# One adaLN decode block: three weight and cache loads merged away, and the matmuls without a reader changed from bf16 to f32

## The chip, the cores and the metric

The kernel runs on one core of a Trainium2 chip. The metric is the device time of one execution in microseconds (us). Before the change it is 187.02 us, the median of three runs (186.99 to 187.12).

## The reference, cut to what matters

Two tokens (B = 2, one position each) of width D = 640 go through an adaLN-conditioned block: a modulation vector, an attention step over the last W = 1024 positions of a cache (32 heads of Dh = 192), and a gated MLP of width F = 1536.

```python
mod = (silu(c) @ w_mod).reshape(2, 6, 1, 640)      # sa, ca, ga, sb, cb, gb
h = layernorm(x) * (1 + ca) + sa
q = (h @ wq)                                       # 640 -> 32*192
scores = einsum('bhqd,bhkd->bhqk', q, k) * Dh ** -0.5
o = einsum('bhqk,bhkd->bhqd', softmax(scores), v)
x = x + ga * (o @ wo)                              # 32*192 -> 640
h = layernorm(x) * (1 + cb) + sb
out = x + gb * ((gelu(h @ w_gate) * (h @ w_up)) @ w_down)
```

All inputs are bf16. Nearly all bytes are read once: 25.2 MB of K and as much of V, 7.9 MB each of wq and wo, 4.9 MB of w_mod, and 5.9 MB of the three MLP matrices.

## The kernel before, in words

**How it is scheduled.** The program is written out as one list of operations per engine. `_Sched` records each operation with the buffers it reads and writes; when the lists are emitted, an operation waits for the counters of those that it depends on. Each engine works through its list strictly in order, so the order in which the code below calls `S.op` and `S.dma` is the order on each engine. All transfers are issued by SP (SyncE), on one hardware queue, also in order: a transfer whose buffer is not yet free holds up all transfers behind it.

**Buffers.** `ring` has four slots of one tile each (a tile is 64 positions x 192 for each of 128 partitions, 3 MB); `r1` is large enough for wq, and later holds two tiles (slots 4 and 5), and later wo. `items` lists the cache transfers as (kind, batch, first tile, number of tiles, slot, semaphore). `load_kv(n)` issues the items up to n at that place of SP's list.

**Scores** (lines 554 to 561). For each batch b, tile t and half hf, VectorE multiplies the half tile of K in place by the query (`d_mul`, L465), TensorE sums over the head dimension with twelve matmuls against an identity matrix (`p_reduce`, L476), and VectorE reduces the rest from PSUM (`d_rows`, L483). Between the halves TensorE has `filler()`: matmuls whose result nobody reads (L454). They write bank 4, which nobody needs at that time.

**Weighted values.** After the two softmaxes VectorE makes a masked copy of the weights for each tile (`d_mask`, L511), and TensorE multiplies it with the V tile (`p_pv`, L523, 32 matmuls). Batch 1's last two V tiles go into slots 2 and 3, which held batch 0's first two V tiles: each is issued when the matmuls of the tile that it replaces are done.

**Projection and MLP.** `normalize` (L536, L540), `p_sel` (L548) and three transposes (L597) bring the attention output into the form `oT`. wo arrives in pieces of `WO_SPLIT` row groups out of 48; after each piece come its matmuls (L628), 4 for each row group. Then the second layer norm: its statistics need one f32 matmul (L369), and it ends in a transpose to `hT` (L358). Then gate (L646), up (L646), and down (L669) in pieces of `WD_SPLIT`, and the output.

**Matmuls without a reader.** `warm(n, bk)` puts n matmuls on TensorE's list, in bf16, 128 x 128 weights (`ident_b`) against 384 columns (`qbc`). `WO_WARM`, `WU_WARM` and `WD_WARM` say how many follow each piece, and there are fixed calls around `p_sel`, before gate, and before up. In all there are 120 of them.

The order around the V tiles, the layer norm and the MLP, as TensorE's list has it: PV of batch 1's four tiles, `p_sel(0)`, warm, `p_sel(1)`, warm, wo pieces each with their warm matmuls, statistics matmul, warm, gate, warm, up, warm, down in three pieces with warm after the first.

Of the kernel before, what the change touches and what calls it, by code (L numbers as in the profile page):

```python
# [103 lines left out]
def bass_adaLN_cond__sliding_block_cached__geglu_ffn__decode_kernel(  # L104
# [17 lines left out]
    _, H, Sk, Dh = A_k_cache.shape  # L122
# [9 lines left out]
    DN = D // NJ  # L132
# [21 lines left out]
    NS = 4  # L154
    SL = J * Dh
    WQ_SPLIT = [5]
    assert sum(WQ_SPLIT) == KT
    WO_SPLIT = [16, 16, 12, 4]
    OT_SPLIT = [16, 16, 16]
    assert sum(WO_SPLIT) == NT and sum(OT_SPLIT) == NT  # L160
    WU_SPLIT = [5]
    assert sum(WU_SPLIT) == KT
    WD_SPLIT = [6, 4, 2]
    assert sum(WD_SPLIT) == FT
    ND = 4

    WO_WARM = [0, 8, 0, 9]
    WU_WARM = [5]
    WD_WARM = [5, 0, 0]

    es = ExitStack()
    with es:
        S = _Sched(nc, es)
# [21 lines left out]
        def tile_f(slot, n=1):  # L195
            if slot < NS:
                return ring_f[:, slot * SL:(slot + n) * SL]
            return r1[:, (slot - NS) * SL:(slot - NS + n) * SL]
# [11 lines left out]
        qbc = sb("qbc", [P, 2, Dh], BF16)  # L210
        ident_b = sb("ident_b", [P, P], BF16)
        ident_f = sb("ident_f", [P, P], F32)
# [15 lines left out]
        modC = sb("modC", [P, 6, DN], F32)  # L228
# [19 lines left out]
        ps = es.enter_context(nc.psum_tensor("ps", [P, 8, 512], F32))  # L248
# [4 lines left out]
        BK_W = 4  # L253
# [5 lines left out]
        def bank(k):  # L259
            return ("bank", k)  # L260
# [4 lines left out]
        sem_wq = [S.sem("d_wq%d" % i) for i in range(len(WQ_SPLIT))]  # L265
        sem_wo = [S.sem("d_wo%d" % i) for i in range(len(WO_SPLIT))]
        sem_wg = S.sem("d_wg")
        sem_wu = [S.sem("d_wu%d" % i) for i in range(len(WU_SPLIT))]
        sem_wd = [S.sem("d_wd%d" % i) for i in range(len(WD_SPLIT))]
        sem_ring = [S.sem("d_ring%d" % i) for i in range(4)]  # L270
        sem_out = S.sem("d_out")

        def k_dma(dst, src):
            return lambda e: e.dma_start(dst, src)  # L274
# [5 lines left out]
        def dram_rows(v):  # L280
# [9 lines left out]
             reads=[("S", 0, 0, 0), ("S", 0, 0, 1), ("S", 0, 1, 0), ("S", 0, 1, 1)], writes=["ident_f"], name="ident_f")  # L290
        S.op("pool", lambda e: e.tensor_copy(out=ident_b[:, :], in_=ident_f[:, :]),
             reads=["ident_f"], writes=["ident_b"], name="ident_b")
# [3 lines left out]
             reads=["ident_f"], writes=["G32"], name="G32")  # L296
        S.op("dve", lambda e: e.tensor_reduce(out=M32[:, :], in_=ident_f[:, :].rearrange("p (h t) -> p h t", t=QP), axis=AX.X, op=ALU.add),
             reads=["ident_f"], writes=["M32"], name="M32")
# [3 lines left out]
             reads=["G32"], writes=["Bsel"], name="Bsel")  # L302
# [3 lines left out]
             reads=["M32"], writes=["DS"], name="DS")  # L306


        for b in range(2):
            S.op("dve", (lambda b: lambda e: e.tensor_copy(  # L310
                out=SEL[:, b, :, BS * b:P:SQ], in_=G32[:, :].rearrange("p (j m) -> p m j", m=HM)))(b),
                reads=["G32"], writes=["SEL"], name="SEL%d" % b)
        for b in range(2):
            for m in range(HM):
# [3 lines left out]
                    reads=["ident_f"], writes=["Qsel"], name="Qsel%d%d" % (b, m))  # L318
# [4 lines left out]
        def ring_keys(slot):  # L323
            return [half_key(slot, 0), half_key(slot, 1)]
# [9 lines left out]


        items = [("k", 0, 0, 2, 0, 0), ("k", 0, 2, 2, 2, 1), ("k", 1, 0, 2, NS, 2), ("k", 1, 2, 2, 0, 0), ("v", 0, 0, 2, 2, 1),
                 ("v", 0, 2, 2, NS, 2), ("v", 1, 0, 2, 0, 0), ("v", 1, 2, 1, 2, 1), ("v", 1, 3, 1, 3, 3)]
        place = {(kind, b, t0 + i): slot + i for kind, b, t0, nt, slot, _ in items for i in range(nt)}
        assert NTL == 4 and len(place) == 4 * NTL

# [3 lines left out]
        def load_kv(upto, deps=()):  # L344
            while keep["kv"] < upto:
                kind, b, t0, nt, slot, sm = items[keep["kv"]]
                cache = A_v_cache if kind == "v" else A_k_cache
                S.dma("sp", k_dma(tile_f(slot, nt),
                                  cache[b, :, K0:Sk, :].rearrange("h (q r) d -> h q r d", q=QP)[:, :, J * t0:J * (t0 + nt), :].rearrange("h q r d -> h q (r d)")),
                      sem_ring[sm], writes=[k for i in range(nt) for k in ring_keys(slot + i)], deps=deps, name="ld_%s%d_%d" % (kind, b, t0))  # L350
                keep["kv"] += 1
# [98 lines left out]
        def warm(n, bk):  # L450
            def f(e):
                last = None
                for _ in range(n):
                    last = e.matmul(ps[:, bk, 0:2 * Dh], lhsT=ident_b[:, :], rhs=qbc[:, :, :].rearrange("p b d -> p (b d)"),  # L454
                                    start=True, stop=True)
                return last
            if n:
                S.op("pe", f, reads=["ident_b", "qbc"], writes=[bank(bk)], name="warm")

        def filler(n=1):  # L460
            warm(n * ND, BK_W)

        def d_mul(b, t, hf):
            ks = slot_of("k", b, t)
# [66 lines left out]
        def normalize(b):  # L531
            for g in range(NJ):
                rows = slice(SQ * g, SQ * (g + 1))
                cols = slice((g % 2) * Dh, (g % 2 + 1) * Dh)
                if g % 2 == 0:
                    S.op("act", (lambda rows, cols: lambda e: e.activation(out=On[rows, b, :], in_=ps[rows, BK_O, cols], func=ACTF.Identity,  # L536
                                                                           scale=rden[rows, b:b + 1]))(rows, cols),
                         reads=[bank(BK_O), ("rden", b)], writes=[("On", b, g)], name="On%d_%d" % (b, g))
                else:
                    S.op("dve", (lambda rows, cols: lambda e: e.tensor_scalar(out=On[rows, b, :], in0=ps[rows, BK_O, cols],  # L540
                                                                              scalar1=rden[rows, b:b + 1], scalar2=None, op0=ALU.mult))(rows, cols),
                         reads=[bank(BK_O), ("rden", b)], writes=[("On", b, g)], name="On%d_%d" % (b, g))

        def p_sel(b):
            def f(e):
                last = None
                for m in range(HM):
                    last = e.matmul(ps[:, BK_H + m // 2, (m % 2) * Dh:(m % 2 + 1) * Dh], lhsT=SEL[:, b, m, :], rhs=On[:, b, :],  # L548
                                    start=(b == 0 and m % 2 == 0), stop=(b == 1), skip_group_check=True)
                return last  # L550
            S.op("pe", f, reads=["SEL"] + [("On", b, g) for g in range(NJ)], writes=[bank(BK_H + c) for c in range(NQC)], name="sel%d" % b)


        def scores(b, ta, tb):
            for t in range(ta, tb):
                for hf in range(2):
                    d_mul(b, t, hf)
                    filler()
                    p_reduce(b, t, hf)
                    if (b, t, hf) != (0, 0, 0):  # L560
                        d_rows(*((b, t, 0) if hf else (b, t - 1, 1) if t else (b - 1, NTL - 1, 1)))

        def weighted(b, ta, tb):
            for t in range(ta, tb):
                d_mask(b, t)
                p_pv(b, t)
# [10 lines left out]
        softmax(0)  # L577
        softmax(1)
        weighted(0, 0, 2)
        load_kv(9)  # L580
        weighted(0, 2, 4)
        normalize(0)
        for t in range(NTL):
# [2 lines left out]
            if t == NTL - 1:  # L586
                p_sel(0)
        normalize(1)
        warm(3, 1)
        p_sel(1)  # L590
        warm(6, 1)
        assert keep["kv"] == len(items)
        for c in range(NQC):
            move(("act", "dve")[c % 2], oc[:, QC * c:QC * (c + 1)], ps[:, BK_H + c, 0:QC], [bank(BK_H + c)], [("oc", c)], "oc%d" % c)
# [1 line left out]
        for i, nt in enumerate(OT_SPLIT):  # L596
            S.op("dve", (lambda t0, nt: lambda e: e.transpose(oT[:, t0:t0 + nt, :], oc.rearrange("p (q k) -> p k q", k=NT)[:, t0:t0 + nt, :]))(t0, nt),  # L597
                 reads=[("oc", c) for c in range(NQC)], writes=[("oT", t) for t in range(t0, t0 + nt)], name="oT%d" % i)
            t0 += nt

        wo_src = A_wo.rearrange("(p t) n -> p t n", t=NT)
        wo_of = [(sum(WO_SPLIT[:i]), sum(WO_SPLIT[:i + 1])) for i in range(len(WO_SPLIT))]
        for i, (ta, tb) in enumerate(wo_of):
# [5 lines left out]
              writes=["wg"], deps=r3_dead, name="ld_wg")  # L609
# [13 lines left out]
        for i, (ta, tb) in enumerate(wo_of):  # L623
            def f(e, ta=ta, tb=tb):
# [6 lines left out]
            S.op("pe", f, reads=[("wo", i)] + [("oT", t) for t in range(ta, tb)], writes=[bank(BK_M)], name="wo%d" % i)  # L631
            warm(WO_WARM[i], 1)

        S.op("dve", lambda e: e.tensor_tensor(out=lnt[:, 0, :], in0=ps[:, BK_M, 0:DN], in1=modC[:, 2, :], op=ALU.mult),
             reads=[bank(BK_M), ("modC", 0)], writes=[("lnt", 0)], name="ga_attn")
        S.op("dve", lambda e: e.tensor_tensor(out=X2[:, 0, :], in0=lnt[:, 0, :], in1=X2[:, 0, :], op=ALU.add),
             reads=[("lnt", 0)], writes=[("X2", 0)], name="x1")
        layer_norm("ln2", 1, 3)
        warm(12, 1)

        def ffn_gu(bk, wv, key, name, ka, kb):
            def f(e):
# [6 lines left out]
            S.op("pe", f, reads=["hT", key], writes=[bank(bk)], name="ffn_" + name)  # L649

        ffn_gu(BK_G[0], wg_v, "wg", "wg", 0, KT)
        warm(8, 1)
        S.op("act", lambda e: e.activation(out=gl, in_=ps[:, BK_G[0], 0:FN], func=ACTF.Gelu_apprx_tanh),
             reads=[bank(BK_G[0])], writes=["gl"], name="gelu")
        k0 = 0
        for ci, nk in enumerate(WU_SPLIT):
            ffn_gu(BK_G[1], wu_v, ("wu", ci), "wu%d" % ci, k0, k0 + nk)
            k0 += nk
            warm(WU_WARM[ci], 1)
        S.op("dve", lambda e: e.tensor_tensor(out=aC[:, :], in0=ps[:, BK_G[1], 0:FN], in1=gl, op=ALU.mult),  # L660
             reads=[bank(BK_G[1]), "gl"], writes=["aC"], name="geglu")
        to_contraction(aT[:, :, :], aC[:, :], FT, ["aC"], ["aT"], "aT")
        f0 = 0
        for ci, nf in enumerate(WD_SPLIT):
            def f(e, f0=f0, nf=nf):
# [6 lines left out]
            S.op("pe", f, reads=["aT", ("wd", ci)], writes=[bank(BK_C)], name="down%d" % ci)  # L672
            warm(WD_WARM[ci], 1)
            f0 += nf

        S.op("dve", lambda e: e.tensor_tensor(out=lnt[:, 1, :], in0=ps[:, BK_C, 0:DN], in1=modC[:, 5, :], op=ALU.mult),
             reads=[bank(BK_C), ("modC", 1)], writes=[("lnt", 1)], name="gb_y")
        S.op("dve", lambda e: e.tensor_tensor(out=sc[:, :], in0=lnt[:, 1, :], in1=X2[:, 0, :], op=ALU.add),
             reads=[("lnt", 1), ("X2", 0)], writes=["sc"], name="outC")
# [36 lines left out]
```

## Time and profile before

| | before |
|---|---|
| time, median of three runs | 187.02 us |
| the profiled execution: its own time | 187.01 us |
| its span, first to last instruction | 185.7 us |
| granted TensorE clock, mean | 0.915 of full speed |
| DMA: bytes, mean rate | 77.02 MB, 415 GB/s |
| VectorE busy | 106.6 us (57%) |
| TensorE matmuls busy | 117.2 us (63%) |
| warm matmuls (L454) | 24.7 us, 120 of 339 ns each |
| ScalarE busy, GpSimd busy | 13.9 us, 4.9 us |

The profile is of one execution. The 1.31 us between its span and its time lie outside the instructions. A line such as "L454 PE MATMUL" names the line of the kernel, the engine and the operation. "PEld" is the load of the stationary operand, which runs beside matmuls. The record of a matmul includes its way through the array, so that one record of 339 ns does not mean that the next starts 339 ns later. The granted clock is full (1.0) or half (0.5) at each moment of this trace.

### The profile page before, as it was taken

How to read it: one execution, taken by the hardware profiler on the slowest of the kernel's cores; microseconds unless marked ns; L12 is line 12 of the kernel's file. 1: busy time of each engine (PE TensorE's matmuls, PEld its weight loads, DVE VectorE, ACT ScalarE, POOL GpSimd, SP SyncE). 2: the span in 40 equal slices, each digit the busy share in tenths (PEclk: the TensorE clock that was granted, in tenths of full speed). 3: DMA queues.
4: the chain of work that ended last, by engine and by line, in shares of the span. 5: the costliest groups of instructions: out<-in, count | busy, mean ns of one | idle time of the engine just before them, and what ended most of it. 6: DMA issues, size and time to landing. Idle time of an engine off the chain costs nothing.

```text
span 185.7 us, 2254 instructions
## 1 busy us (share of the span) xinstructions
PE 117.2 (63%) x1014; PEld 60.8 (33%) x1014; DVE 106.6 (57%) x114; ACT 13.9 (7%) x24; POOL 4.9 (3%) x12
## 2 busy tenths in 40 slices
PE   0004500871079899988999885349928977299844
PEld 0001200440024334433344342226614654265422
DVE  6801600020598999999999993294556714803331
ACT  2001400013000000000000000200010004100400
POOL 8200000000000000000000000000000000000000
PEclk9999999998559999999999999558996999859999
DMA  7999998898999989899999989899999999999991
GB/s 248 414 437 477 463 463 389 371 491 371 487 413 434 468 381 459 381 487 402 455 424 434 459 381 466 381 487 413 395 434 424 424 435 424 413 408 435 422 392 50
DMA packets 2925, 77.02 MB, mean 415 GB/s; under 512 B 356, under 2 KB 356, under 8 KB 868
## 3 DMA queue, kind: packets, MB, share of 16 engines
q1 hardware_dynamic: 2916, 76.88, 96.7%
q8 instruction: 8, 0.13, 0.3%
q14 instruction: 1, 0.01, 0.0%
HBM read 76.88 MB, written 0.00 MB: 414 GB/s over the span
## 4 chain that ended last, share of the span: by engine, by line
DMA 43%; DVE 36%; PE 16%; SPq 1%; ACT 1%; issue 1%; POOL 1%; DVEq 0%; POOLq 0%
DMA ring<-in_A_k_cache_dram 24%; DVE ring L465 19%; DMA ring<-in_B_w_down_dram 18%; PE ps L523 10%; DVE r L465 7%; DVE Sg L483 5%; PE ps L476 4%; DVE Em L511 2%; SPq L274 1%; ACT E_sb L502 1%; PE ps L504 1%; PE ps L498 1%; DVE On L540 0%; ACT On L536 0%; PE ps L491 0%
## 5 line engine op out<-in xcount | busy, mean ns | idle before, releaser
L465 DVE TENSOR_TENSOR ring<-ring,qbc 128x6144 bf16<-128x6144 bf16 x12 | 40.1, 3351 | 8.4 <-DMA ring<-in_A_k_cache_dram 8.4
L476 PE MATMUL ps<-ring,ident_b 128*128 128x512 bf16 x144 | 34.7, 393 | 13.0 <-DVE ring L465 13.0
L454 PE MATMUL ps<-qbc,ident_b 128*128 128x384 bf16 x120 | 24.7, 339 | 0.7 <-ACT qbc L432 0.7
L523 PE MATMUL ps<-ring,Em 128*64 128x384 bf16 x192 | 19.6, 371 | 7.8 <-DVE Em L511 6.6
L476 PEld LDWEIGHTS ps<-ring,ident_b 128*128 128x128 bf16 x144 | 13.6, 100 | 32.7 <-DVE ring L465 17.2
L511 DVE TENSOR_TENSOR Em<-E_sb,M32b 128x2048 bf16<-128x2048 bf16 x8 | 18.1, 2288 | 5.5 <-PE ps L523 5.5
L523 PEld LDWEIGHTS ps<-ring,Em 128*64 128x64 bf16 x192 | 12.4, 125 | 14.6 <-DVE Em L511 7.3
L454 PEld LDWEIGHTS ps<-qbc,ident_b 128*128 128x128 bf16 x120 | 11.6, 101 | 10.9 <-issue 2.8
L401 PE MATMUL ps<-ring,scT 128*32 128x480 bf16 x40 | 4.4, 601 | 16.0 <-DVE scT L358 16.0
L465 DVE TENSOR_TENSOR r<-r,qbc 128x6144 bf16<-128x6144 bf16 x4 | 13.4, 3352 | 0.0
L483 DVE TENSOR_REDUCE Sg<-ps 128x32 f32<-128x512 f32 x16 | 11.0, 687 | 3.4 <-PE ps L476 3.4
L424 PE MATMUL ps<-r,hT 128*32 128x384 bf16 x80 | 5.8, 475 | 10.7 <-DMA r<-in_A_wq_dram 10.7
L476 PE MATMUL ps<-r,ident_b 128*128 128x512 bf16 x48 | 11.1, 380 | 1.8 <-DVE r L465 1.8
L434 DVE CAST aux<-ps 128x384 bf16<-128x384 f32 x4 | 2.0, 553 | 16.6 <-PE ps L424 15.7
L628 PE MATMUL ps<-r,aux 128*32 128x160 bf16 x192 | 5.1, 271 | 4.4 <-DMA r<-in_A_wo_dram 2.6
L424 PEld LDWEIGHTS ps<-r,hT 128*32 128x32 bf16 x80 | 3.2, 135 | 13.8 <-issue 11.6
L476 PEld LDWEIGHTS ps<-r,ident_b 128*128 128x128 bf16 x48 | 4.4, 98 | 8.1 <-DVE r L465 3.4
L401 PEld LDWEIGHTS ps<-ring,scT 128*32 128x32 bf16 x40 | 1.2, 132 | 17.5 <-DVE scT L358 16.0
L540 DVE TENSOR_SCALAR On<-ps,rden 32x192 bf16<-32x192 f32 x4 | 1.7, 418 | 8.9 <-ACT On L536 8.9
L502 ACT ACTIVATE E_sb<-Sg,nb 128x256 bf16<-128x256 f32 x2 | 1.0, 507 | 75.6 <-DVE nb L501 75.6
L628 PEld LDWEIGHTS ps<-r,aux 128*32 128x32 bf16 x192 | 4.3, 114 | 5.8 <-DMA r<-in_A_wo_dram 3.6
L523 PE MATMUL ps<-r,Em 128*64 128x384 bf16 x64 | 5.4, 327 | 0.0
(73 smaller groups left out, 65.6 us busy)
## 6 DMA issues: line engine op xcount, KB each, us to landing
ring<-in_A_k_cache_dram SPq DMA_DIRECT2D x3, 6144.0 KB, 40.3
ring<-in_A_v_cache_dram SPq DMA_DIRECT2D x2, 6144.0 KB, 23.3
r<-in_A_wq_dram SPq DMA_DIRECT2D x1, 7680.0 KB, 30.7
r<-in_A_k_cache_dram SPq DMA_DIRECT2D x1, 6144.0 KB, 38.4
r<-in_A_v_cache_dram SPq DMA_DIRECT2D x1, 6144.0 KB, 23.3
ring<-in_A_v_cache_dram SPq DMA_DIRECT2D x2, 3072.0 KB, 17.6
r<-in_A_wo_dram SPq DMA_DIRECT2D x2, 2560.0 KB, 23.7
ring<-in_w_mod_dram SPq DMA_DIRECT2D x1, 4800.0 KB, 14.2
```

The lines of the kernel that those rows point to most:

```text
L274: return lambda e: e.dma_start(dst, src)
L401: last = e.matmul(ps[SQ * j:SQ * j + SQ, bk, 0:3 * DN].rearrange("p (i n) -> p i n", i=3), lhsT=scT[:, k, :], rhs=wm_v[:, k, 3 * part * D: ...
L424: last = e.matmul(ps[SQ * j:SQ * j + SQ, BK_H + c, 0:QC], lhsT=hT[:, k, :], rhs=wq_v[:, k, RN * j + QC * c:RN * j + QC * (c + 1)], start=( ...
L434: S.op("dve", lambda e: e.tensor_copy(out=dst, in_=src), reads=reads, writes=writes, name=name)
L454: last = e.matmul(ps[:, bk, 0:2 * Dh], lhsT=ident_b[:, :], rhs=qbc[:, :, :].rearrange("p b d -> p (b d)"), start=True, stop=True)
L465: S.op("dve", lambda e: e.tensor_tensor(out=tile_v(ks)[:, hf * JH:(hf + 1) * JH, :], in0=tile_v(ks)[:, hf * JH:(hf + 1) * JH, :], in1=qbc[ ...
L476: last = e.matmul(o_ap, lhsT=ident_b[:, :], rhs=tile_v(ks)[:, hf * JH:(hf + 1) * JH, ci * GC:(ci + 1) * GC], start=(ci == 0), stop=(ci == ...
L483: S.op("dve", lambda e: e.tensor_reduce(out=S_sb[:, b, a:a + JH], in_=ps[:, hf, 0:JH * GC].rearrange("p (j c) -> p j c", j=JH), axis=AX.X, ...
L502: S.op("act", lambda e: e.activation(out=E_sb[:, b, :], in_=S_sb[:, b, :], func=ACTF.Exp, scale=SCALE, bias=nb[:, 0:1], accum_out=esum[:, ...
L511: S.op("dve", lambda e: e.tensor_tensor(out=Em[:, t % 2, :, :], in0=E_sb[:, b, J * t:J * (t + 1)].unsqueeze(2).broadcast_to([P, J, H]), in ...
L523: last = e.matmul(ps[r:r + 2 * H, BK_O, 0:ON], lhsT=Em[:, t % 2, 2 * jp:2 * jp + 2, :].rearrange("p j c -> p (j c)"), rhs=tile_v(vs)[:, 2 ...
L628: last = e.matmul(ps[SQ * j:SQ * j + SQ, BK_M, 0:DN], lhsT=oT[:, t, :], rhs=wo_v[:, t, DN * j:DN * j + DN], start=(t == 0), stop=(t == NT ...
```

## The change

It does three things.

1. Batch 1's last two V tiles come in one transfer of 6 MB into slots 2 and 3 in place of two of 3 MB. It is issued when both tiles that it replaces are done, and both of its tiles wait for all of it.
2. wo comes in two pieces, of 32 and 16 row groups, in place of four of 16, 16, 12 and 4.
3. A matmul without a reader is now f32: 128 x 128 weights (`ident_f`) against 480 columns of `modC`. Four of the bf16 matmuls give way to one of these, with rounding: after the wo pieces 0, 8, 0, 9 become 2, 2; after up 5 becomes 1, after the first piece of down 5 becomes 1; the fixed calls go from 3, 6, 12 and 8 to 1, 1, 3 and 2; each of the 16 fillers between scores goes from four to one. In all 120 become 29.

```diff
-    WO_SPLIT = [16, 16, 12, 4]
+    WO_SPLIT = [32, 16]
...
-    ND = 4
-
-    WO_WARM = [0, 8, 0, 9]
-    WU_WARM = [5]
-    WD_WARM = [5, 0, 0]
+
+    WO_WARM = [2, 2]
+    WU_WARM = [1]
+    WD_WARM = [1, 0, 0]
...
-        sem_ring = [S.sem("d_ring%d" % i) for i in range(4)]
+        sem_ring = [S.sem("d_ring%d" % i) for i in range(3)]
...
-                 ("v", 0, 2, 2, NS, 2), ("v", 1, 0, 2, 0, 0), ("v", 1, 2, 1, 2, 1), ("v", 1, 3, 1, 3, 3)]
+                 ("v", 0, 2, 2, NS, 2), ("v", 1, 0, 2, 0, 0), ("v", 1, 2, 2, 2, 1)]
...
-                    last = e.matmul(ps[:, bk, 0:2 * Dh], lhsT=ident_b[:, :], rhs=qbc[:, :, :].rearrange("p b d -> p (b d)"),
+                    last = e.matmul(ps[:, bk, 0:3 * DN], lhsT=ident_f[:, :], rhs=modC[:, 0:3, :].rearrange("p i n -> p (i n)"),
...
-                S.op("pe", f, reads=["ident_b", "qbc"], writes=[bank(bk)], name="warm")
+                S.op("pe", f, reads=["ident_f", ("modC", 0)], writes=[bank(bk)], name="warm")
 
         def filler(n=1):
-            warm(n * ND, BK_W)
+            warm(n, BK_W)
...
-        load_kv(9)
+        load_kv(8)
...
-        warm(3, 1)
+        warm(1, 1)
         p_sel(1)
-        warm(6, 1)
+        warm(1, 1)
...
-        warm(12, 1)
+        warm(3, 1)
...
-        warm(8, 1)
+        warm(2, 1)
```

## The prediction

> **What bounds the kernel now.** I read the page first: which resource has no holes, and what the chain that ended last is made of. Columns of the slices: tenths of busy time in 40 slices; of the queue: packets, MB, share of 16 engines.
>
> ```profile
> DMA  7999998898999989899999989899999999999991
> q1 hardware_dynamic: 2916, 76.88, 96.7%
> DMA ring<-in_A_k_cache_dram 24%; DVE ring L465 19%; DMA ring<-in_B_w_down_dram 18%; PE ps L523 10%; DVE r L465 7%; DVE Sg L483 5%; PE ps L476 4%; DVE Em L511 2%; SPq L274 1%; ACT E_sb L502 1%; PE ps L504 1%; PE ps L498 1%; DVE On L540 0%; ACT On L536 0%; PE ps L491 0%
> ```
>
> The transfer engines are busy from the second slice to the last but one, and no compute engine is. The chain names VectorE and TensorE in the middle, but they only decide when SP may issue; it ends in a 33.92 us wait for the last piece of w_down. The second view is the chain in order of time, its end:
>
> ```profile
> 148.89 33.92 DMA ring<-in_B_w_down_dram
> 182.81 0.04 issue
> 182.85 0.35 PE ps L669 x8
> ```
>
> So the last byte lands at 182.81, and 2.9 us of the span follow. A change pays if the stream of transfers ends earlier, and costs if compute is not ready for its last piece. The third view is the timeline of the tail (start, us, engine line; in brackets the idle time before and who ended it):
>
> ```profile
> 150.84 2.79 PE L523 MATMUL ps<-ring,Em 128*64 128x384 bf16 x32 [1.14 <-DMA ring<-in_A_v_cache_dram]
> ...
> 162.78 2.33 PE L628 MATMUL ps<-r,aux 128*32 128x160 bf16 x64 [2.41 <-DMA r<-in_A_wo_dram]
> ...
> 169.00 0.46 PE L628 MATMUL ps<-r,aux 128*32 128x160 bf16 x16 [0.21 <-DMA r<-in_A_wo_dram]
> ...
> 171.37 2.11 PE L454 MATMUL ps<-qbc,ident_b 128*128 128x384 bf16 x12
> ...
> 174.09 1.00 PE L646 MATMUL ps<-ring,hT 128*32 128x384 bf16 x20 [0.61 <-DVE hT L358]
> 175.02 1.47 PE L454 MATMUL ps<-qbc,ident_b 128*128 128x384 bf16 x8
> ...
> 178.18 1.00 PE L646 MATMUL ps<-ring,hT 128*32 128x384 bf16 x20 [1.69 <-DMA ring<-in_B_w_up_dram]
> ```
>
> Every stage of the tail waits for a transfer; the tightest slack is the 1.69 us before up. The clock by stages (us; PE and PEld busy; clock in the column after POOL):
>
> ```profile
> 147.40:150.85 3.45, 2.31 (x32) 1.40 (x27) 2.06 (x1) 0.00 (x0) 0.00 (x0) 1.00 1.01 425
> 157.70:161.10 3.40, 1.29 (x64) 1.12 (x64) 3.40 (x3) 0.83 (x1) 0.00 (x0) 0.99 0.98 417
> 161.10:164.50 3.40, 1.72 (x55) 1.72 (x59) 0.51 (x1) 0.00 (x0) 0.00 (x0) 0.50 0.99 413
> ```
>
> 2.31 us of work in 3.45 kept the full clock; 1.29 in 3.40 was followed by half clock.
>
> **Three transfers fewer.** The trace's records of single packets (median duration) price them. Of a transfer's 128 packets an engine carries 8, then a semaphore packet of 9 ns. A V packet of 24,576 bytes takes 0.9155 us, one of 49,152 takes 1.816: the merge saves 8 x (2 x 0.9155 - 1.816) + 0.009 = 0.129 us. wo's 15,360 and 5,120 bytes take 0.577 and 0.198, 20,480 takes 0.766: 8 x 0.009 + 0.009 = 0.081. The 40,960-byte packet is not in the trace; between 38,400 bytes (1.420) and 49,152 it is 1.514: 8 x (2 x 0.766 - 1.514) + 0.009 = 0.153. Sum 0.36 us of each engine, and since the queue has no holes all of it moves the last landing. Bounds: 0.22 if the new packet size saves only its semaphore, 0.5 if an unseen few ns lie between packets.
>
> SP issues the merged V after batch 0's second tile, at about 130.6, where the first of the pair went out one tile (2.6 us) earlier. The transfer ahead, issued at 113.52, lands 23.3 us later (the page's median), at about 136.8, so the queue does not run dry: 5 us or more of cover. Behind it on SP stand the wo transfers, which are issued at 135.84 in any case.
>
> **Both V tiles wait for 150.8.** The third PV tile ran from about 147.1 beside the last landing; now it starts at 150.8 with the fourth. One tile is 2.4 us at full clock, 4.5 at half (the tile at 139.99, after 4.18 us of idling). TensorE now idles from 147.1 to 150.8, 3.7 us, so the first 3.4 us may run at half clock: PV ends at 155.9 to 157.3 instead of 153.6. Behind it TensorE's list holds `p_sel`, warm and wo. oT began 3.9 us after PV; two transposes (1.42 each) are needed for the first 32 groups: ready at 162.6 to 164.0. That wo piece lands where the second did, 162.7. So the merge is hidden, or costs 1.3 here.
>
> **wo in two pieces.** First piece: 128 matmuls at half clock (64 in 2.01) 4.0 us, to 166.6 to 168.0; two f32 matmuls to 168.2 to 169.7. The second lands at 168.95 - 0.36 = 168.6, and now has 64 matmuls (1.12 at full clock, 0.17 to the end of the last) where 16 were left: done at 170.0 to 171.0, against 169.46. This is 0.5 to 1.5 late into the layer norm, which nothing but the slack before up covers.
>
> **f32 matmuls.** The trace has none with many columns except the transposes of L491 (128 columns): 270 ns at full clock, 372 at half. The 102 ns between are twice what 128 bf16 columns would differ by (0.42 ns a column, from twelve 512-column matmuls in 2.60 us, against 0.83): two column times each. An f32 matmul that is no transpose is two records (L369: x4 for two calls). So 2 x 2 x 480 x 0.42 = 0.81 us, against 0.65 for four bf16. Below: 0.40, if a record streams at bf16's rate; above: 1.1, if its two weight loads (0.30 us the pair at 171.13) are not hidden, as bf16's are. I take 0.81, as L491 is the nearest row. Between scores a half has 2.60 of reduction in a VectorE period of 3.87, so 1.27 us are free: hidden at any of these prices.
>
> In the tail, on the path: the statistics come 1.62 after wo's end, 171.6 to 172.6; two f32 (1.6) fit. hT 2.9 later, at 174.6 to 175.5; three f32 (2.4) fit. Gate 0.93, two f32 1.6: up can start at 177.1 to 178.1. It lands at 178.15 - 0.36 = 177.8. From up's start to the last piece of down are 2.6 (geglu, transpose), 0.53, one f32 0.8, 0.35: 4.3, and that piece lands at 182.45: up may start as late as 178.15 at no cost. It fits with nothing to spare at the late end. **The sum:** the profiled execution has 187.01; minus 0.36 is 186.65, and the median 187.02 gives 186.66.
>
> **Rivals.**
> 1. *The f32 matmul takes 1.1 us (slower).* Decisive above about 0.9. From 164.0: wo to 168.0, two f32 170.2, wo's second 171.4, two f32 173.6 (statistics wait for them), 173.9, three f32 177.2 (past hT), gate 178.1, two f32 180.3, up 181.2, f32 182.3, aT at 182.9, down 0.53, f32 1.1, last 24 matmuls 0.5: 185.0 against 183.05 before. Some 1.9 us: 188.9. For it: f32 weight loads take 0.15 each at full clock, bf16's 0.08. Against: loads run ahead of the matmul before.
> 2. *The f32 matmuls hold the clock less (slower).* Then the tail runs at half clock from 164: f32 1.6 us each, wo's second piece 2.2, gate and up 1.8. The same sum ends near 193.5, 10 us late: 197; with the clock lost for one or two stretches of 3.4 us, 188 to 192. Against: between scores 2.6 of 3.87 us remain bf16, 67%, the share that held at 147.40. For it: from 174.70 to 178.15 the warm matmuls are most of the work. The Trainium skill (TensorE: Matmul & The Clock Gate, on the clock gate) has half clock after an idle window of some 3.4 us. The trace is stricter, since 1.29 busy of 3.40 was already too little; the late ends of the sum have the merged V tiles at half clock for that.
> 3. *Part of the slack is overrun.* At f32 0.9 or half clock at one more place, up starts 0.3 to 0.7 past 178.15: 186.8 to 187.3.
> 4. *Each transfer has a cost of its own on the path.* The Trainium skill (DMA: Bandwidth & Descriptors, on the anatomy of one DMA) gives about 2 us fixed per DMA on GpSimd's path, which for three would be an estimate of 6 us, 181 in all; the trace does not bear it out. As a mechanism here: gaps between transfers. The five from 169.00 to 182.81 carry 5.9 MB, 427 GB/s, so no such gap is seen. If there were 0.2 us at each, the time would be 186.66 - 0.6 = 186.1.
>
> **How the numbers follow.** 0.2% is 0.37 us, about what a measurement of this kernel can tell from no change. The forecast case (0.52) ends at 186.65 give or take 0.1, on that very bound: half faster, half the same. Rival 1 has 0.28, rival 2 0.08, rival 3 0.08 (same), rival 4 0.02, a score stage at half clock 0.02 (twelve matmuls 5.1 and f32 1.6 make 6.7 a half, 16 x 2.8 = 45 us on VectorE's chain, some 35 past the queue's backlog). Faster 0.27 + 0.02 = 0.29, same 0.25 + 0.08 = 0.33, slower 0.38. The likeliest case's own range is 186.5 to 186.8; the range to 188.9 takes in rivals 1 and 3 and leaves out some 0.13.
>
> **What would show it.** Right: the last w_down piece landing 0.3 to 0.4 earlier with 2916 - 3 x 144 = 2484 packets on q1; L454 records (58) starting 0.4 us apart in the tail; PV's last 64 in one run from 150.7; up still released by its transfer. Wrong: up or down released by TensorE's own list (L454 before them), a clock of 0.50 after 168, or a hole in the DMA row near 135.

## The result, and the profile after

The changed kernel takes 187.59 us, the median of 14 runs, from 187.25 to 189.39. The kernel before takes 187.14 beside it (186.88 to 187.26). It is slower by 0.45 us at the median, and far less even than before. The ratio of the means is 1.0040, with a 95% interval of 1.0026 to 1.0054. Such ratios, here and below, are of means, which a few long executions move more than a median, and they leave out executions over 1.5% above the fastest of their kernel. The profiled execution has 187.55, a span of 186.3, 0.6 more than before.

The page of the changed kernel, the lines that answer to those shown of before:

```profile
DMA  7999998899998989999898989989899999999980
q1 hardware_dynamic: 2484, 76.88, 96.3%
DMA ring<-in_A_k_cache_dram 25%; DVE ring L464 19%; DMA ring<-in_A_v_cache_dram 11%; PE ps L522 8%; DVE r L464 7%; DVE Sg L482 5%; PE ps L475 4%; PE ps L453 3%; PE ps L627 3%; DVE aux L596 2%; DVE Em L510 1%; PE ps L645 1%; ACT E_sb L501 1%; PE ps L503 1%; PE ps L668 1%
```

The packets went as counted (2484), but w_down, 18% of the chain before, is gone from it. In its place stand V (11%), the f32 matmuls (L453, 3%) and wo's (L627, 3%). The lines are one lower than before, since a line was removed. The chain in order of time, its end:

```profile
164.63 4.00 PE ps L627 x125
168.62 1.81 PE ps L453 x4
170.43 1.22 PE ps L627 x64
171.65 1.81 PE ps L453 x4
173.46 0.26 PE ps L368 x2
...
176.28 1.00 PE ps L645 x20
177.28 1.81 PE ps L453 x4
179.09 0.95 PE ps L645 x20
...
182.23 1.00 PE ps L453 x2
183.23 0.56 PE ps L668 x24
```

No transfer is left in this end: TensorE goes from piece to piece, and four groups of f32 matmuls (L453) stand among them. The timeline of TensorE where that run begins, the row of two tiles at full clock in the kernel before, and the line of the f32 matmuls of the changed kernel (min/median/max ns):

```profile
150.77 7.07 PE L522 MATMUL ps<-ring,Em 128*64 128x384 bf16 x64 [3.58 <-DMA ring<-in_A_v_cache_dram]
```

```profile
130.41 5.39 PE L523 MATMUL ps<-r,Em 128*64 128x384 bf16 x64
```

```profile
L453 PE MATMUL ps<-modC,ident_f x58: 566/566/670, 41.7 to 182.7; 128*128 128x480 f32 x58
```

The last two PV tiles start together after 3.58 us of idling and take 7.07 us, where two tiles took 5.39 in the kernel before, at a granted clock of 1.00. The last landing of w_down, at 183.13 by the trace, is 0.3 later than before, not 0.36 earlier, and yet TensorE is not waiting for it: its f32 matmuls end at 183.23. Had TensorE been ready, the last eight matmuls (0.35) would have ended at 183.5, where they ended at 183.20 before; they ended at 183.79. So of the 0.6 that the span grew, 0.3 is there by the stream alone, and the chain on TensorE, which sets the end, adds the rest.

### The profile page after: what moved, and what is told of

Read it like the earlier page. It is cut to its first block, busy times and chain, and to the rows that moved or that the text cites. A ratio compares the mean times of both kernels' runs of the same rounds, so it can differ in the third digit from the quotient of the medians.

```text
span 186.3 us, 2125 instructions
## 1 busy us (share of the span) xinstructions
PE 121.5 (65%) x952; PEld 61.9 (33%) x952; DVE 106.6 (57%) x114; ACT 13.9 (7%) x24; POOL 4.9 (3%) x12
## 3 DMA queue, kind: packets, MB, share of 16 engines
q1 hardware_dynamic: 2484, 76.88, 96.3%
## 4 chain that ended last, share of the span: by engine, by line
DVE 39%; DMA 35%; PE 21%; ACT 1%; issue 1%; POOL 1%; SPq 0%; DVEq 0%; POOLq 0%
DMA ring<-in_A_k_cache_dram 25%; DVE ring L464 19%; DMA ring<-in_A_v_cache_dram 11%; PE ps L522 8%; DVE r L464 7%; DVE Sg L482 5%; PE ps L475 4%; PE ps L453 3%; PE ps L627 3%; DVE aux L596 2%; DVE Em L510 1%; PE ps L645 1%; ACT E_sb L501 1%; PE ps L503 1%; PE ps L668 1%
## 5 line engine op out<-in xcount | busy, mean ns | idle before, releaser
L453 PE MATMUL ps<-modC,ident_f 128*128 128x480 f32 x58 | 28.0, 578 | 0.0
L522 PE MATMUL ps<-ring,Em 128*64 128x384 bf16 x192 | 21.2, 393 | 10.2 <-DVE Em L510 6.6
L522 PEld LDWEIGHTS ps<-ring,Em 128*64 128x64 bf16 x192 | 14.0, 132 | 17.1 <-DVE Em L510 7.1
L453 PEld LDWEIGHTS ps<-modC,ident_f 128*128 128x128 f32 x58 | 10.3, 190 | 5.3 <-issue 2.8
L627 PE MATMUL ps<-r,aux 128*32 128x160 bf16 x192 | 5.3, 289 | 3.3 <-DVE aux L596 3.3
L627 PEld LDWEIGHTS ps<-r,aux 128*32 128x32 bf16 x192 | 4.9, 124 | 4.7 <-issue 4.7
```

What stands on the lines that cost most here:

```text
L453: last = e.matmul(ps[:, bk, 0:3 * DN], lhsT=ident_f[:, :], rhs=modC[:, 0:3, :].rearrange("p i n -> p (i n)"), start=True, stop=True)
L522: last = e.matmul(ps[r:r + 2 * H, BK_O, 0:ON], lhsT=Em[:, t % 2, 2 * jp:2 * jp + 2, :].rearrange("p j c -> p (j c)"), rhs=tile_v(vs)[:, 2 ...
L627: last = e.matmul(ps[SQ * j:SQ * j + SQ, BK_M, 0:DN], lhsT=oT[:, t, :], rhs=wo_v[:, t, DN * j:DN * j + DN], start=(t == 0), stop=(t == NT ...
```

## The experiments

Each time stands beside runs of the kernel before on the same chip, whose medians were 187.00 to 187.08.

**The three edits apart.**

V's last two tiles in two transfers again, the rest as changed:

```diff
-                 ("v", 0, 2, 2, NS, 2), ("v", 1, 0, 2, 0, 0), ("v", 1, 2, 2, 2, 1)]
+                 ("v", 0, 2, 2, NS, 2), ("v", 1, 0, 2, 0, 0), ("v", 1, 2, 1, 2, 1), ("v", 1, 3, 1, 3, 3)]
```

> The changed kernel with V's last two tiles in two transfers again. Theory (the merged V sends both tiles to 150.8, TensorE idles into half clock, and from there an unbroken chain of TensorE and VectorE work sets the end): the chain is 4 us shorter, up waits for its transfer again, and the two wo transfers saved are left: 186.9, that is 0.2 below the kernel before (187.14). Rival (the f32 matmuls or the wo split cost the time by themselves): it stays at 187.4 to 187.6.

Measured 186.88 (186.77 to 187.16), ratio 0.9993 [0.9984, 1.0002]. Neither the f32 matmuls nor the wo split cost any time without the merged V. But the mechanism was not quite the expected one: in its profile up landed at 178.10 and started at 178.31, behind TensorE's own list, and only the last eight matmuls waited for their transfer again (182.76). The slack behind up took the 0.2.

bf16 matmuls in the changed kernel (8 and 9 behind wo's pieces, 3, 6, 12, 8, 5, 5 elsewhere):

```diff
-                    last = e.matmul(ps[:, bk, 0:3 * DN], lhsT=ident_f[:, :], rhs=modC[:, 0:3, :].rearrange("p i n -> p (i n)"),
+                    last = e.matmul(ps[:, bk, 0:2 * Dh], lhsT=ident_b[:, :], rhs=qbc[:, :, :].rearrange("p b d -> p (b d)"),
```

> The changed kernel with four bf16 matmuls of 384 columns for each f32 one. Theory: the chain from 150.8 remains, but it has four stations where two f32 take 1.81 against 1.3 of eight bf16, about 1.2 us less before up; up would be ready at 177.9, before its transfer (178.5): 186.8 to 187.1. Rival (the merged V alone is too late for any fillers): 187.4 or more.

Measured 187.78 (186.82 to 189.23), ratio 1.0050 [1.0025, 1.0075]. The theory fell here: without the f32 matmuls the median is no lower, and in the profiled execution (188.74) the chain ends in w_down, landing at 184.62. The stream itself was late, by 1.8 us. Three of the twelve executions (186.82, 187.12, 187.13) do lie below the lowest of the changed kernel (187.25), so bf16 may help where the stream is in time; this run does not show it.

V merged alone (point 1 of the change and nothing else), in the kernel before:

> The kernel before with only V's last two tiles merged. Theory: PV ends at 157.8, wo's end is 0.7 late, and the slack before up (1.7 us) takes it: 187.0, 0.1 below the kernel before, with more spread. Rival (the merge alone costs it): 187.4 or more.

Measured 187.80 (186.78 to 189.90), ratio 1.0036 [1.0013, 1.0059]. The rival holds: the merge alone costs this much, and it makes executions differ by 3 us.

wo in two pieces alone:

```diff
-    WO_SPLIT = [16, 16, 12, 4]
+    WO_SPLIT = [32, 16]
...
-    WO_WARM = [0, 8, 0, 9]
+    WO_WARM = [8, 9]
```

> The kernel before with only wo in 32 and 16 (eight and nine bf16 matmuls behind the pieces). Theory: the last piece has 64 matmuls behind it in place of 16, 0.85 us, taken by the slack before up; the stream ends 0.23 earlier by the packet prices: 186.9. Rival A (64 matmuls behind the last piece show): 187.4 or more. Rival B (the last landing is set by the slowest of 16 engines and does not move by what is saved on the mean engine): 187.1.

Measured 186.87 (186.71 to 187.04), ratio 0.9990 [0.9981, 0.9998]: 0.13 less than the runs beside it, between the theory (0.23 less) and its rival B (nothing).

The f32 matmuls alone (point 3):

> The kernel before with only the f32 matmuls (wo in four pieces with 0, 2, 0, 2 behind them). Theory: 0.9 us each against 0.65, hidden between scores and in the slack of the tail: within 0.1 of the kernel before. Rival (the f32 matmuls cost the time by themselves): 187.4 or more.

Measured 186.89 (186.76 to 187.09), ratio 0.9994 [0.9985, 1.0002]. They have no cost of their own.

**What a transfer costs.** wo in 24 transfers:

```diff
-    WO_SPLIT = [16, 16, 12, 4]
+    WO_SPLIT = [2] * 24
...
-    WO_WARM = [0, 8, 0, 9]
+    WO_WARM = [0] * 15 + [8] + [0] * 7 + [9]
```

> The kernel before with wo in 24 transfers of two row groups. It measures the price of a transfer: by the packet prices wo takes 24 x (8 x 0.102 + 0.009) = 19.8 us of each engine in place of 18.5, and the end comes 1.3 us later: 188.4. Rival (a transfer has no price on the path): 187.1. Rival (each costs far more, 0.5 us or so): 197.

Measured 188.47 (188.26 to 188.54), ratio 1.0078 [1.0065, 1.0091]: 1.4 us for 20 transfers more, where the packet records say 1.3.

**TensorE's part.** Four f32 matmuls where TensorE waits for the merged V:

```diff
                 p_pv(1, t)
+            if t == 1:
+                warm(4, 1)
```

> The changed kernel with four f32 matmuls more, behind the second PV tile of batch 1, where TensorE waits 3.6 us for the merged V. Theory: the last two PV tiles run at full clock and end at about 155.7 in place of 157.8, wo's first piece starts on its transfer, and the chain is off the path: 186.9 to 187.1. Rival (half clock there is not what makes the chain late): 187.4 or more.

Measured 187.21 (186.83 to 189.26), ratio 1.0031 [1.0007, 1.0055]. In the profiled execution (187.01) the two tiles took 5.39 and up waited for its transfer again, as the theory has it. But the median is 0.1 above what it gave, and the spread did not go.

No matmuls behind the wo pieces (`WO_WARM = [0, 0]`):

> The changed kernel without the f32 matmuls behind the two wo pieces (two and two left out; nobody reads them). Theory: they stand in the chain, 1.8 us behind the first piece and 0.2 in front of the statistics, so up is ready 1.8 or more earlier and waits for its transfer: 186.9 to 187.1. Rival (they keep the clock): wo's second piece and what follows run at half clock, 187.6 to 189.

Measured 188.27 (186.82 to 190.65), ratio 1.0047 [1.0022, 1.0072]. A miss, and mixed with the lateness below. The profile shows the rival's mechanism: a granted clock of 0.64 from 172 to 176, where the changed kernel has 1.00. So the two pairs left out here hold the clock; in the changed kernel the same pairs stand in the chain.

**The late stream.** The packets of the merged V showed what the theory lacked. In the kernel before, the 16 transfer engines finish the V transfer ahead one by one, from 133.6 to 135.4; the next one was issued at 128.0. With V merged it is issued at 130.8 to 132.0, and in the profiled executions of five kernels with it 3 to 21 packets from 133 to 139 took 0.2 to 2 us longer than the median of their size. The only other such burst is at 2 us, when the first transfer starts. So a new theory: issued too late.

All profiles of this case, the later ones too, fall in line by the time of this issue. Call a packet long when it took over 0.2 us more than the median of its size. Issued up to 129.2, there is one long packet from 131 to 141 (nine kernels); from 130.8 to 131.2 there are 3 to 5 (the changed kernel and two others, with the last landing at 182.88 to 183.13); from 131.3 to 132.0 there are 14 to 21 (three kernels, 183.22 to 184.62); at 134.6 there are 15, behind a gap (one kernel, 185.44). Where the issue waits for batch 0's second V tile on TensorE, its time follows the granted clock from 126 to 130: 0.87 and 0.83 where it came at 130.8, 0.78 at 131.3, 0.66 at 131.9. The kernel before, and V merged alone (the column behind five engines' busy times is the granted clock):

```profile
126.00:130.00 4.00, 4.00 (x46) 2.67 (x44) 1.93 (x1) 0.00 (x0) 0.00 (x0) 0.89 1.05 455
```

```profile
126.00:130.00 4.00, 4.00 (x36) 2.44 (x34) 1.11 (x2) 0.00 (x0) 0.00 (x0) 0.66 0.97 418
```

With 0.89 that tile was done at 130.6, with 0.66 at 131.9. That is a likely reason why executions of one kernel differ so much, but not a shown one: each kernel has one profiled execution.

Two tests take lateness and merging apart.

The pair stays in two transfers, but both are issued after the second tile's matmuls, in the kernel before:

```diff
-        load_kv(9)
+        load_kv(9, deps=[keep["pv", 0, 1]])
```

> The kernel before, V's last two tiles still in two transfers, but the first of them also waits for the second tile's matmuls, so that both are issued at about 131 as the merged one is. New theory (late issue: the leading transfer engines finish the V transfer ahead at 133.5, and the packets of a transfer that is issued only 2 us before that come late, as at the start of the kernel): 187.3 to 188 with a spread of 2 us, like the merged V alone (187.8). Rival (size of the transfer, or both tiles waiting for all of it): 187.0 with a spread of 0.4, as before.

Measured 188.22 (187.12 to 189.54), ratio 1.0061 [1.0037, 1.0086]. Late issue alone, without any merging, costs 1.2, a little more than the theory's upper end; the rival is out. (The profiled execution, 187.12, is one of the quick ones: issued at 130.8, four long packets, last landing at 183.00.)

Both wait for the third tile:

```diff
-        load_kv(9)
-        weighted(0, 2, 4)
+        load_kv(7)
+        weighted(0, 2, 3)
+        load_kv(9, deps=[keep["pv", 0, 2]])
+        weighted(0, 3, 4)
```

> The kernel before with V's last two tiles in two transfers that both wait for batch 0's third tile of matmuls, so that they are issued at about 133.5, when the leading transfer engines run out of work. If late issue is the cause, the cost grows with the lateness: 2.6 us later than the pair that waits for the second tile, up to 2.6 us more: 189.5 to 190.5. Rival (the spread has another cause): 187.0 to 188.2.

Measured 189.74 (189.56 to 189.77), ratio 1.0147 [1.0131, 1.0162]. With the latest issue (134.6 in its profile) the cost is largest and the spread is gone. In the profiled execution all 16 engines were idle before the first packets at 135.9; that it is so in every execution would explain the even times, but is not shown.

V merged alone, but issued earlier, by moving the second softmax behind batch 0's V tiles:

```diff
         softmax(0)
-        softmax(1)
...
         weighted(0, 2, 4)
+        softmax(1)
         normalize(0)
```

> The kernel before with only the V tiles merged, and the second softmax behind batch 0's four V tiles. New theory: the merged V alone cost 187.8 by late packets; issued early it ends at 186.9 with a spread of 0.4. Rival (the merge itself costs): 187.4 or more with a spread of 2 us.

Measured 186.88 (186.74 to 187.07, one at 188.00), ratio 0.9999 [0.9989, 1.0009]: the merge issued at 128.7 costs nothing, where issued at 131.9 it cost 0.8. (The second softmax moved without the merge was not run.) By stages (us; the columns as above, then the busy share of the transfer engines and GB/s). The kernel before:

```profile
133.00:135.00 2.00, 2.00 (x30) 1.41 (x28) 0.00 (x0) 0.00 (x0) 0.00 (x0) 1.00 0.82 340
135.00:137.00 2.00, 0.81 (x10) 0.33 (x6) 0.41 (x1) 0.68 (x2) 0.00 (x0) 1.00 0.91 393
```

V merged alone, issued at 131.9:

```profile
133.00:135.00 2.00, 2.00 (x29) 1.28 (x25) 1.27 (x1) 0.00 (x0) 0.00 (x0) 1.00 1.12 377
135.00:137.00 2.00, 2.00 (x27) 1.25 (x22) 0.00 (x0) 0.00 (x0) 0.00 (x0) 1.00 0.81 246
```

The pair issued at 134.6:

```profile
133.00:135.00 2.00, 2.00 (x28) 1.28 (x26) 1.27 (x1) 0.00 (x0) 0.00 (x0) 1.00 0.21 82
135.00:137.00 2.00, 2.00 (x28) 1.25 (x22) 0.00 (x0) 0.00 (x0) 0.00 (x0) 1.00 0.74 197
```

V merged and issued at 128.7:

```profile
133.00:135.00 2.00, 1.38 (x15) 0.71 (x9) 0.49 (x2) 0.00 (x0) 0.00 (x0) 1.00 0.86 369
135.00:137.00 2.00, 0.48 (x3) 0.37 (x2) 0.72 (x3) 0.90 (x3) 0.00 (x0) 0.77 0.97 418
```

A packet is booked whole in the stretch in which it starts, so single stretches jitter. But 246 GB/s (V merged alone) and 82 and 197 (the pair at 134.6) are a hole, and in both kernels the rest of the stream carries it to the end: the last landing is at 184.61 and 185.44, against 182.81.

**Both causes together.** The changed kernel with the second softmax moved:

> The changed kernel with the second softmax moved behind batch 0's four V tiles, so that the merged V is issued some 3.8 us earlier (127); nothing is left out. New theory: no late packets, so the spread goes, and what is left is the chain of TensorE work from 150.6 on: 187.2 to 187.6, none over 187.8. Rival (lateness has nothing to do with the spread): 187.2 to 189.4 as the changed kernel. Rival (there is no chain and lateness is all): 186.8.

Measured 187.40 (186.70 to 188.66), ratio 1.0019 [1.0004, 1.0033]. The chain is left: in the profiled execution V was issued at 128.6 (127 expected), there was no burst of late packets, V landed at 150.51 and w_down at 182.92, yet the span was 187.4. That execution is the one at 188.66, beyond what I had allowed: the half clock held for two stretches of 3.4, and PV took 8.28.

The same with the four f32 matmuls in the wait:

> The same, with four f32 matmuls more behind the second PV tile of batch 1, where TensorE waits for the merged V. New theory (two causes, late packets and a half clock in the last two PV tiles that pushes the chain past the transfers): both are gone, 186.7 with a spread of 0.4, 0.36 below the kernel before. Rival (the half clock is not what makes the chain late): 187.4.

Measured 186.91 (186.69 to 187.11), ratio 0.9991 [0.9983, 1.0000]. Cost and spread are gone; the 186.7 that the theory gave was not reached. The clock behind V's landing, without the four matmuls (two rows) and with them:

```profile
150.60:154.00 3.40, 3.35 (x22) 2.25 (x24) 0.00 (x0) 0.00 (x0) 0.00 (x0) 0.50 0.95 410
154.00:157.50 3.50, 3.50 (x32) 2.35 (x29) 0.00 (x0) 0.00 (x0) 0.00 (x0) 0.63 1.13 484
```

```profile
150.60:154.00 3.40, 3.40 (x33) 1.82 (x33) 0.15 (x1) 0.00 (x0) 0.00 (x0) 1.00 0.92 398
```

And with bf16 in place of f32 throughout:

> All three transfers saved, four bf16 matmuls in place of each f32 one, the second softmax behind batch 0's V tiles, and twenty bf16 matmuls where TensorE waits for the merged V. If both causes are gone and the f32 matmuls are not a third: 186.9 with a spread of 0.4, as with f32 (186.91). Rival (f32 costs or brings something): off by over 0.3.

Measured 186.84 (186.72 to 187.19), ratio 0.9992 [0.9983, 1.0001]. Where both causes are gone, f32 or bf16 makes no difference that shows.

## Why the prediction was wrong, step by step

**What bounds it, and the packet prices: held.** The kernel before ends with its stream of transfers, and the price of a transfer held where it was magnified (1.4 us measured for 1.31 priced). The saving of 0.36 on a mean engine did not come through whole: kernels with three saved and nothing late (186.91, 186.84) are 0.11 and 0.16 below the kernel before; the one with f32 alone, which saves none, is 0.19 below. In the traces the last landing of the first two is 182.83 and 182.60, against 182.81: the slowest of the 16 engines sets it. Averaged over the 16, the last piece does end 0.37 and 0.38 earlier in them (181.57 and 181.56 against 181.94), though one execution each shows it, and that of f32 alone has 0.13 too. Why the slowest moves less than the mean stays open.

**"5 us or more of cover": the step that failed.** I took the cover from the median landing of a V transfer, 136.8; in that trace the transfer ahead landed at 135.9. And a landing is that of the slowest engine: the leading ones were done at 133.6. An issue is also not a first packet: where the pair was issued at 134.6, packets began at 135.9 and came at full pace from 137.4. Issued at 130.8 to 132.0, the leading engines had 2.8 to 1.6 us of work left, where the prediction had 5 or more, and whether that suffices differs from execution to execution. So the sum's minus 0.36 did not come: in the profiled execution the last landing is 0.32 later. I named a hole near 135 as what would prove me wrong, and gave it no case and no chance. It costs 0.8 us at the median in the V merge alone.

**Both V tiles wait for 150.8: held, a little short.** PV ended at 157.8 (said: 155.9 to 157.3). The half clock was one stretch of 3.4 (150.9 to 154.3), as said, but two tiles at full clock take 5.4, not twice 2.4.

**f32 at 0.81: mis-sized.** Two take 1.81 in the chain, 0.91 each. Their four records start 0.40 apart, as priced, but the second starts 0.51 behind the first, and the next matmul 0.50 behind the last: some 0.2 more for each group. Rival 1's price (1.1, weight loads fully exposed) was wrong, they are mostly hidden; but 0.91 is just past the 0.9 from which the prediction called it decisive. Rival 2 (the clock not held) was wrong too: the tail of the changed kernel has a granted clock of 1.00 from 168 on.

**"It fits with nothing to spare": it did not.** The late end of the sum had wo's second piece done at 171.0 and up ready at 178.1; measured were 171.65 and 179.09. PV gave 0.5 of this, the f32 pairs behind wo's first piece and behind gate 0.2 each, and the rest is rounding. The pair in front of the statistics added nothing: the first record of their matmul started at 173.32, 0.05 behind its input, as before. (The expectation of the run without matmuls behind wo counts 0.2 for it.) This is rival 3, to which I gave 0.08; up was 0.9 past 178.15, more than its 0.3 to 0.7. A sum whose own late end has no slack left should not have carried 0.52.

The measured 187.59 does lie below the 188.9 of the prediction's range, but that end was drawn for rival 1's price. A late stream had no part in it, so this is luck.

So two costs come from the merged V, whose transfer went later and whose tiles both wait for it. The first needs nothing else. The second, the chain on TensorE, needs the wo split or the f32 matmuls beside it: V merged and issued early in the kernel before costs nothing (186.88), and the changed kernel with the early issue has 187.40. Which of the two it needs, or whether both, no run separates. The profiled execution of the changed kernel has both: the chain sets its end, and the stream without it would have cost 0.3 of the 0.6. In the slowest executions (188.62 to 189.39) the first is probably larger; these were not profiled.

## What to carry to other kernels

A queue that looks full runs dry at its leading engine (133.6 here), not at the landing that the profile gives, which is the last engine's (135.9); take the cover from there and subtract the time from issue to first packet (1.3 where the pair was issued at 134.6). Joining two transfers moves the issue to the later release and the first use to the later landing: price both, and look whether an engine idles long enough in between to lose its clock. Before merging, look for work that can move out of the way of the release, as the softmax here.

## What the runs showed of the hardware that was not expected

The engines of one stream drift apart by almost 2 us: one transfer's 16 parts ended between 133.6 and 135.4. The first packets of a transfer that was issued 1.6 to 2.8 us before the leading engine was done were slow in part, up to 2 us over a median of 1.8 for 49,152 bytes, and so are those at the start of the program, up to 1.5 over a median of 1.4 for 38,400 bytes. f32 matmuls of 480 columns count for the clock: four of them in the wait for V kept the granted clock at 1.00, where it was 0.50 without them.
